# A gMLP that has its gated rows turned by DMA, a third buffer of turned rows, and a filler inside Wo

## The chip, the cores and the metric

One core of one Trainium2 chip. The metric is the device time of one execution in microseconds (us), as a median of runs; all runs here were in the fast state, but for one single run whose state is unknown. A ratio says how one kernel stands to the kernel before, which was run in the same rounds on the same chip: it is the estimate from the runs of both (within 0.0005 of the ratio of their means), so not quite the ratio of the medians quoted beside it. Where I turn a ratio into microseconds, I multiply its distance from 1 by the median of the kernel before in those rounds.

## The reference, cut to what matters

The program applies, twice, a recurrent attention with memory (A) and a gMLP (B), each on layer-normalised rows and each added to its input. To "turn" a tile is to transpose it.

```python
# A: 64 segments of 32 tokens; each sees 8 memory rows which the segment before it wrote
for s in range(n_seg):
    h = jnp.concatenate([mem, xs], axis=1)
    q, k, v = ...                                   # h @ Wq, Wk, Wv
    o = softmax(mask(q k^T * scale)) @ v
    o = jnp.einsum('bhte,hed->btd', o, Wo)
    mem = o[:, :M, :].copy()                        # the recurrence
    ...
# B
z  = _gelu(jnp.einsum('bsd,df->bsf', x, w_in))      # "the projection"
z1 = z[..., :Fh];  z2 = _layernorm(z[..., Fh:])
g  = jnp.einsum('ts,bsf->btf', w_sp, z2) + b_sp     # "the gate", a mix over tokens
return jnp.einsum('bsf,fd->bsd', z1 * g, w_out)     # "w_out"
```

S = 2048 tokens are 16 tiles of 128 rows; Fh = 688.

## The kernel before, the parts that count

In B, the projection takes turned rows from two buffers, a pair of tiles in each; VectorE makes statistics and ScalarE normalises.

```python
def load_rows(self, q):
    lo = KT * FF + 2 * KT * P * (q % 2)             # two buffers
    t = self.take(lo, 2 * KT * P).rearrange(...)
    self.nc.sync.dma_start_transpose(out=t, in_=self.xb_d[2 * P * q:2 * P * (q + 1), :]...)
...
for tt in range(NT):
    project(tt)                                     # 12 matmuls, two gelus on ScalarE, statistics on VectorE
    ...
    if tt % 2 == 1:
        if tt // 2 + 2 < NT // 2:
            front.load_rows(tt // 2 + 2)
        norms(tt // 2, {5: (NT - 4, NT - 3), 9: (NT - 2, NT - 1)}.get(tt, ()))   # late rows of A
        if tt > 1:
            normalise(tt - 3)
            normalise(tt - 2)
```

The gate stage, a tile at a time: 32 gate matmuls into `pg`, a product with z1 on VectorE (`u`), six PE transposes of `u` and two ScalarE copies (`uT`), six matmuls with w_out (`py`).

```python
for t in range(2, NT):
    if t > 2:
        gate(t, range(0, 8))
    turn_u(t - 1)                # six transposes on TensorE
    gate(t, range(8, 13))
    finish(t - 1)                # w_out
    gate(t, range(13, NT))
    product(t)                   # issues the next spatial weight (512 KB, turned by DMA), then u
```

In A, the segments form a chain, and TensorE's waits in it are filled with work that does not belong to it: projections of the next tile's edge rows (`psb`), or Wo of older rows (`pwB`). `fill()` takes the next piece. A segment ends so:

```python
fill()                           # third filler: eight matmuls, two quarters of a psb chunk
... Rm, Rt ...                   # ScalarE: logarithms and exponentials of the sums
for r in range(2):
    nc.vector.tensor_tensor(out=hview(uT_cur[:], r, 0, 8), ...)   # what Wo waits for
    ...
pw = accB.tile([P, 512], F32, name="pw")
wo_pass(pw, uT_cur)              # Wo: 128 small matmuls; writes the memory rows
build_hA(s + 1, pw)
...
fill()                           # fourth filler: sixteen matmuls
```

The softmax here doesn't subtract the row's maximum and nothing guards it: scores larger than these inputs give would overflow.

## Time and profile before

| | before |
|---|---|
| median of 3 runs | 1899.3 us (1897.0 to 1901.9) |
| profiled execution, span | 1886.2 us |
| recurrent block, start to first projection matmul | 800.2 us, then 763.4 us |
| projection, first to first gate matmul | 48.2 us, then 50.4 us |
| gate stage, first gate matmul to start of the last w_out | 110.2 us, then 108.8 us |

Each part of the table is the distance between two starts in TensorE's timeline. TensorE is busy nearly all the time, so these stages simply add up, and a change shows in the stage that it changes. One warning ahead, as it matters later: the profiled execution took 1887.9 us by the clock that times the runs, 9 us less than the fastest of the three.

### The profile page before, as it was taken

Reading aid. Unit: us, or ns where it says so; the run is one execution under the profiler, and the core shown is the slowest. Engines: PE = TensorE matmul, PEld = TensorE weight load, DVE = VectorE, ACT = ScalarE, POOL = GpSimd, SP = SyncE. Lnnn points to the kernel's source line nnn. Section 1 sums busy time; section 2 is a strip of 40 time slices with the busy share of each in tenths; the row PEclk is TensorE's granted clock in tenths of the full one; section 3 lists DMA queues with packets and bytes.
Section 4 is the critical chain, followed back from the end, with each engine's and each line's share of the span. In section 5 each row is a group of like instructions: output and inputs, shape, how many; then the busy total and the mean of one; then the engine's idle time right before and its main releaser. Section 6 shows DMA issues by size and latency. Waiting matters only on the chain.

```text
span 1886.2 us, 94665 instructions
## 1 busy us (share of the span) xinstructions
PE 1761.7 (93%) x43776; PEld 1019.3 (54%) x43776; DVE 1157.8 (61%) x2700; ACT 1139.4 (60%) x2134; POOL 136.8 (7%) x285
## 2 busy tenths in 40 slices
PE   2999999999999999889989999999999999998898
PEld 1555555555555555435545555555555555554455
DVE  2666666676667766584346666666766676666622
ACT  1667766666676666562236776666766676665411
POOL 5000000000000000022010000000000000002000
PEclk9999999999999999999989999999999999999999
DMA  9100000021002101278630000001200120125463
GB/s 349 46 21 19 19 18 18 19 79 30 19 22 76 36 25 32 84 157 161 157 116 21 22 21 21 22 22 46 80 21 21 52 78 25 28 71 148 109 138 95
DMA packets 165269, 119.93 MB, mean 64 GB/s; under 512 B 111896, under 2 KB 140328, under 8 KB 164872
## 3 DMA queue, kind: packets, MB, share of 16 engines
q1 hardware_dynamic: 143016, 65.11, 14.3%
q0 software_dynamic: 10560, 34.07, 5.5%
q10 hardware_dynamic: 11296, 14.70, 2.7%
q8 instruction: 342, 5.60, 1.2%
q14 instruction: 55, 0.45, 0.1%
HBM read 59.29 MB, written 33.56 MB: 49 GB/s over the span
## 4 chain that ended last, share of the span: by engine, by line
PE 85%; DMA 4%; DVE 4%; issue 3%; ACT 2%; POOL 1%; DVEq 0%; SPq 0%; POOLq 0%; ACTq 0%
PE psm L527 23%; PE pw L582 12%; PE psV L527 12%; PE psb L527 10%; PE pg L321 8%; PE psS L684 5%; PE psO L707 4%; PE pwB L594 3%; PE py L347 2%; PE psD L759 2%; PE psM L749 1%; PE pz L261 1%; DMA y_o<-o_d 1%; DMA Wo_sb<-in_A_Wo_dram 1%; PE pT L338 1%
## 5 line engine op out<-in xcount | busy, mean ns | idle before, releaser
L527 PEld LDWEIGHTS <-hA 128*32 128x32 bf16 x12288 | 303.7, 96 | 310.4 <-DVE hA L638 48.4
L663 ACT CAST rows<-psm 128x512 bf16<-128x512 f32 x512 | 300.3, 587 | 192.2 <-PE psm L527 192.2
L582 PE MATMUL pw<-Wo_sb,uT 128*32 128x128 bf16 x16640 | 268.0, 220 | 39.9 <-issue 29.6
L527 PE MATMUL psm<-Wq_sb,hA 128*32 128x512 bf16 x4096 | 274.5, 381 | 12.4 <-DVE hA L638 9.4
L582 PEld LDWEIGHTS <-uT 128*32 128x32 bf16 x16640 | 237.2, 97 | 89.8 <-DVE uT L769 49.8
L527 PE MATMUL psm<-Wk_sb,hA 128*32 128x512 bf16 x4096 | 269.8, 379 | 0.5 <-ACT rowsB L569 0.5
L527 PE MATMUL psV<-Wv_sb,hA 128*32 128x512 bf16 x4096 | 268.0, 382 | 0.0
L667 DVE STREAM_TRANSPOSE QQ<-rows 128x512 bf16<-128x512 bf16 x256 | 182.1, 711 | 78.2 <-ACT rows L663 77.0
L719 DVE TENSOR_TENSOR uT<-psO,Rt 128x384 bf16<-128x384 f32 x256 | 138.6, 541 | 119.0 <-ACT Rt L772 118.7
L688 ACT ACTIVATE E<-psS 128x448 bf16<-128x448 f32 x256 | 140.0, 547 | 117.8 <-PE psS L684 117.8
L667 DVE STREAM_TRANSPOSE KA<-rows 128x512 bf16<-128x512 bf16 x256 | 181.9, 711 | 37.7 <-ACT rows L663 34.3
L769 DVE TENSOR_TENSOR uT<-psO,Rm 128x128 bf16<-128x128 f32 x256 | 62.5, 286 | 163.2 <-PE psD L759 163.2
L321 PE MATMUL pg<-z2n,wspT 128*128 128x344 bf16 x1024 | 160.1, 310 | 0.0
L772 ACT ACTIVATE Rt<-Rt 128x512 f32<-128x512 f32 x256 | 157.6, 630 | 4.1
L684 PEld LDWEIGHTS <-KA 128*64 128x64 bf16 x2048 | 79.7, 113 | 106.1 <-DVE KA L667 106.1
L767 ACT ACTIVATE Rt<-psD 128x1024 f32<-128x1024 f32 x128 | 131.2, 1025 | 5.9
L527 PEld LDWEIGHTS <-hB 128*32 128x32 bf16 x3072 | 79.4, 97 | 96.8 <-issue 27.3
L321 PEld LDWEIGHTS <-wspT 128*128 128x128 bf16 x1024 | 95.3, 98 | 52.2 <-issue 6.8
L691 DVE TENSOR_TENSOR E<-E,maskN 128x448 bf16<-128x448 bf16 x256 | 95.3, 372 | 41.5 <-ACT E L688 41.5
L527 PE MATMUL psb<-Wq_sb,hB 128*32 128x512 bf16 x1024 | 90.5, 394 | 27.0 <-DVE hB L542 27.0
L684 PE MATMUL psS<-QQ,KA 128*64 128x80 bf16 x2048 | 109.9, 208 | 1.1
L744 ACT CAST VA<-psV 128x512 bf16<-128x512 f32 x128 | 75.1, 586 | 56.5 <-PE psV L527 56.5
(136 smaller groups left out, 2283.9 us busy)
## 6 DMA issues: line engine op xcount, KB each, us to landing
Wo_sb<-in_A_Wo_dram POOLq DMA_DIRECT2D x8, 1024.0 KB, 13.1
xs<-xd ACTq DMA_DIRECT2D x32, 256.0 KB
o_d<-o_sb SPq DMA_DIRECT2D x126, 64.0 KB
y_o<-o_d SPq DMA_DIRECT2D x24, 256.0 KB
xd<-y_o SPq DMA_DIRECT2D x22, 256.0 KB
Wq_sb<-in_A_Wq_dram POOLq DMA_DIRECT2D x8, 512.0 KB, 6.9
Wk_sb<-in_A_Wk_dram POOLq DMA_DIRECT2D x8, 512.0 KB, 11.0
Wv_sb<-in_A_Wv_dram POOLq DMA_DIRECT2D x8, 512.0 KB, 11.4
```

Source lines behind the costliest of these rows:

```text
L321: nc.tensor.matmul(pg[t][:, k, 0:344], lhsT=wsp[t][:, st, :], rhs=z2n[:, st, 344 * k:344 * k + 344], start=(st == 0), stop=(st == NT - 1))
L527: nc.tensor.matmul(ps[32 * cg:32 * cg + 32, :], lhsT=lhs(kt, cg), rhs=rhs(kt, cg), start=(kt == 0), stop=(kt == KT - 1), tile_position=(0, ...
L582: nc.tensor.matmul(po[32 * cg:32 * cg + 32, 0:128], lhsT=lhs[:, n, :], rhs=wo_rhs(h, cg), start=(h == 0), stop=(h == H - 1), tile_position ...
L663: nc.scalar.copy(r[:], ps[:])
L667: nc.vector.transpose(out=QQ[:, j % 2, :, 0:32] if j < 2 else KA[:, j % 2], in_=r[:])
L684: nc.tensor.matmul(pS[64 * g:64 * g + 64, i, c0:80 if K is KA else 112], lhsT=K[:, r, n:n + 2, :].rearrange("p h k -> p (h k)"), rhs=q if ...
L688: nc.scalar.activation(out=E[:, r], in_=pS, func=ACT.Exp, scale=scale)
L691: nc.vector.tensor_tensor(out=E[:, r], in0=E[:, r], in1=maskN[:, j4, :].unsqueeze(1).to_broadcast([P, 4, 112]), op=ALU.mult)
L707: nc.tensor.matmul(o if V is VA else ends(o), lhsT=V[64 * g:64 * g + 64, r, i, :], rhs=E[64 * g:64 * g + 64, r, i, c0:c1].rearrange("p (s ...
L719: nc.vector.tensor_tensor(out=hview(uT_nxt[:], r, 8, 32), in0=oview(r, 8, 32), in1=Rr[:, :, :, 0:24], op=ALU.mult)
L767: nc.scalar.activation(out=Rt[:], in_=psD[:], func=ACT.Ln)
L772: nc.scalar.activation(out=rt, in_=rt, func=ACT.Exp, scale=-1.0)
```

## The change

Three changes in one. Six transposes a tile leave TensorE and become one DMA, issued on the queue of the SP engine behind the next spatial weight, and w_out runs a tile later. The turned rows of the projection get a third buffer, and the late rows come earlier. And four of the eight matmuls of the third filler (one of two, where Wo of old rows is the filler) move into the middle of Wo, where I take the aim to be a bridge over Wo's own pauses.

```diff
-        t = self.take(lo, 2 * KT * P).rearrange("p (kt t) -> p kt t", kt=KT)
+        t = self.take(KT * FF + n * (q % 3), n) if q % 3 < 2 else self.rows.tile([P, DM], F32, name="ln_x")[:].bitcast(BF16)
...
-                if tt // 2 + 2 < NT // 2:
-                    front.load_rows(tt // 2 + 2)
-                norms(tt // 2, {5: (NT - 4, NT - 3), 9: (NT - 2, NT - 1)}.get(tt, ()))
+                if tt // 2 + 3 < NT // 2:
+                    front.load_rows(tt // 2 + 3)
+                norms(tt // 2, {5: (NT - 4, NT - 3), 7: (NT - 2, NT - 1)}.get(tt, ()))
...
             if t + 3 < NT:
                 load_wsp(t + 3)
...
+                uT[t] = up.tile([P, 6, P], BF16, name="uT")
+                nc.sync.dma_start_transpose(out=uT[t][:], in_=u[t][:].rearrange("t (fc s) -> t fc s", s=P))
...
-            turn_u(t - 1)
-            gate(t, range(8, 13))
-            finish(t - 1)
-            gate(t, range(13, NT))
+            gate(t, range(0, 10))
+            finish(t - 2)
+            gate(t, range(10, NT))
             product(t)
+        finish(NT - 2)
         turn_u(NT - 1)          # the last tile keeps its PE transposes
...
-                for kts in ((range(0, 1), range(1, 2), range(2, 4)), (range(0, 4),))[k % 2]:
+                for kts in (((0,), (1,), (2,), (3,)), ((0, 1, 2, 3),))[k % 2]:
...
-                if k in (0, 1, 3):
+                if k < 4:
...
+            wo_pass(pw, uT_cur, range(0, H // 2))
+            fill()
+            wo_pass(pw, uT_cur, range(H // 2, H))
...
-            wo_pass(pw, uT_cur)
```

(Cut: pools that make room for the new buffers, the zeroing of the 80 padding columns of `u`, the order of some loads.)

More of the change, by code (lines that the diff above doesn't have):

```diff
@@ L139, with __init__ @@
 class _Front:
-    def __init__(self, nc, pool, xb_d, w_in):
-        self.nc, self.xb_d, self.w_in = nc, xb_d, w_in.rearrange("(kt p) f -> p kt f", p=P)
+    def __init__(self, nc, pool, rows, xb_d, w_in):
+        self.nc, self.rows, self.xb_d, self.w_in = nc, rows, xb_d, w_in.rearrange("(kt p) f -> p kt f", p=P)
         self.space = pool.tile([P, KT * FF + 4 * KT * P], BF16, name="front")
@@ L156, in load_rows @@
     def load_rows(self, q):
-        lo = KT * FF + 2 * KT * P * (q % 2)
-        t = self.take(lo, 2 * KT * P).rearrange("p (kt t) -> p kt t", kt=KT)
+        n = 2 * KT * P
+        t = self.take(KT * FF + n * (q % 3), n) if q % 3 < 2 else self.rows.tile([P, DM], F32, name="ln_x")[:].bitcast(BF16)
+        t = t.rearrange("p (kt t) -> p kt t", kt=KT)
         self.nc.sync.dma_start_transpose(out=t, in_=self.xb_d[2 * P * q:2 * P * (q + 1), :].rearrange("t (kt s) -> t kt s", s=P))
@@ L231, in b_block @@
         wsp_pool = ctx.enter_context(tc.tile_pool(name="b_wsp", bufs=3))
-        zp = ctx.enter_context(tc.tile_pool(name="b_z", bufs=2))
+        zctx = ExitStack()
+        zp = zctx.enter_context(tc.tile_pool(name="b_z", bufs=2))
         ps_pool = ctx.enter_context(tc.tile_pool(name="b_ps", bufs=1, space=PSUM))
@@ L252, in load_wsp @@
         def load_wsp(t):
-            wsp[t] = wsp_pool.tile([P, NT, P], BF16, name="wspT")
+            wsp[t] = wsp_pool.tile([P, NT, P], BF16, name="wspT", tag="wspT")
             nc.sync.dma_start_transpose(out=wsp[t][:], in_=w_sp[t * P:(t + 1) * P, :].rearrange("t (st s) -> t st s", s=P))
@@ L291, in b_block @@
         late_load(NT - 3, gp.tile([P, DM], F32, name="xs", bufs=3)[:], gp.tile([P, DM], F32, name="xo", bufs=1)[:])
-        late_load(NT - 2, gp.tile([P, DM], F32, name="xs", bufs=3)[:], rows.pool.tile([P, DM], F32, name="ln_x")[:])
+        late_load(NT - 2, *(gp.tile([P, DM], F32, name="xs", bufs=3)[:] for _ in range(2)))
+        wl = wsp_pool.tile([P, 2, DM], F32, name="wspL", tag="wspT")
+        late_load(NT - 1, wl[:, 0, :], wl[:, 1, :])
         for tt in range(NT):
@@ L296, in b_block @@
                 load_wsp((tt - 7) // 2)
-            if tt > 13:
-                load_x(tt - 14)
+            if tt == 14:
+                load_x(0)
             if tt % 2 == 1:
-                if tt // 2 + 2 < NT // 2:
-                    front.load_rows(tt // 2 + 2)
-                norms(tt // 2, {5: (NT - 4, NT - 3), 9: (NT - 2, NT - 1)}.get(tt, ()))
+                if tt // 2 + 3 < NT // 2:
+                    front.load_rows(tt // 2 + 3)
+                norms(tt // 2, {5: (NT - 4, NT - 3), 7: (NT - 2, NT - 1)}.get(tt, ()))
                 if tt > 1:
@@ L305, in b_block @@
                     normalise(tt - 2)
-            if tt == 5:
-                late_load(NT - 1)
         normalise(NT - 2)
         normalise(NT - 1)
+        zctx.close()
+        up = ctx.enter_context(tc.tile_pool(name="b_u", bufs=2))
         if out_final is None:
@@ L314, in b_block @@
         pg, u, uT = {}, {}, {}
+        us = [up.tile([P, 6 * P], BF16, name=f"u{i}", bufs=1) for i in range(2)]
+        for i in range(2):
+            nc.gpsimd.memset(us[i][:, FH:6 * P], 0.0)
         def gate(t, sts):
@@ L327, in product @@
                 load_wsp(t + 3)
-            u[t] = gp.tile([P, FH], BF16, name="u", bufs=1)
-            nc.vector.scalar_tensor_tensor(out=u[t][:].rearrange("p (k f) -> p k f", k=2), in0=pg.pop(t)[:, 0:2, 0:344],
+            u[t] = us[t % 2]
+            nc.vector.scalar_tensor_tensor(out=u[t][:, 0:FH].rearrange("p (k f) -> p k f", k=2), in0=pg.pop(t)[:, 0:2, 0:344],
                                            scalar=c["bsp"][:, t:t + 1], in1=z1[:, t, :].rearrange("p (k f) -> p k f", k=2),
                                            op0=ALU.add, op1=ALU.mult)
-            if t + 2 < NT:
-                load_x(t + 2)
+            if t + 1 < NT:
+                load_x(t + 1)
+                uT[t] = up.tile([P, 6, P], BF16, name="uT")
+                nc.sync.dma_start_transpose(out=uT[t][:], in_=u[t][:].rearrange("t (fc s) -> t fc s", s=P))
         def turn_u(t):
@@ L338, in turn_u @@
                 nc.tensor.transpose(pT[0:fsz, fc * P:(fc + 1) * P], u[t][:, f0:f0 + fsz], ident_bf[:])
-            del u[t]
-            uT[t] = gp.tile([P, 6, P], BF16, name="uT", bufs=1)
+            uT[t] = up.tile([P, 6, P], BF16, name="uT")
             nc.scalar.copy(uT[t][:, 0:5, :].rearrange("p fc r -> p (fc r)"), pT[:, 0:640])
@@ L357, in finish @@
             nc.scalar.dma_start(xd[t * P:(t + 1) * P, :], xo[:])
-            _stats(nc, zp, xo[:], MV_out[:, t, :])
+            _stats(nc, up, xo[:], MV_out[:, t, :])
             _rstd_act(nc, RS_out[:, t:t + 1], MV_out[:, t, 1:2], c)
@@ L368, in b_block @@
         gate(1, range(NT - 2, NT))
-        turn_u(0)
         product(1)
-        gate(2, range(0, 6))
-        finish(0)
-        gate(2, range(6, 8))
         for t in range(2, NT):
-            if t > 2:
-                gate(t, range(0, 8))
-            turn_u(t - 1)
-            gate(t, range(8, 13))
-            finish(t - 1)
-            gate(t, range(13, NT))
+            gate(t, range(0, 10))
+            finish(t - 2)
+            gate(t, range(10, NT))
             product(t)
+        finish(NT - 2)
         turn_u(NT - 1)
@@ L441 @@
         rest()
-    front = _Front(nc, ctx.enter_context(tc.tile_pool(name="front", bufs=1)), xb_d, B_w_in)
+    front = _Front(nc, ctx.enter_context(tc.tile_pool(name="front", bufs=1)), rp, xb_d, B_w_in)
     for blk in range(2):
@@ L770, in segment @@
                                         in1=Rm[:, :, r].rearrange("p g (n q) -> p g n q", q=8), op=ALU.mult)
+            pw = accB.tile([P, 512], F32, name="pw")
+            wo_pass(pw, uT_cur, range(0, H // 2))
+            fill()
+            wo_pass(pw, uT_cur, range(H // 2, H))
+            for r in range(2):
                 rt = Rt[:, :, 256 * r:256 * r + 256]
@@ L776, in segment @@
             tok_out(0)
-            pw = accB.tile([P, 512], F32, name="pw")
-            wo_pass(pw, uT_cur)
             if s + 1 < NSEG:
@@ L826, in tail @@
                     front.load_w(j4)
-                    if j4 > 1:
-                        front.load_rows(j4 - 2)
+                    if j4 > 0:
+                        front.load_rows(j4 - 1)
                 if ys:
```

## The prediction

> **What bounds the kernel now.** I read the page's summary first, then the chain of work that ended last, the table of TensorE's waits, and last the timeline in three places: a recurrent segment, the projection of the gMLP, its gate stage.
>
> ```profile
> PE 1761.7 (93%) x43776; PEld 1019.3 (54%) x43776; DVE 1157.8 (61%) x2700; ACT 1139.4 (60%) x2134; POOL 136.8 (7%) x285
> ...
> q8 instruction: 342, 5.60, 1.2%
> ...
> PE 85%; DMA 4%; DVE 4%; issue 3%; ACT 2%; POOL 1%; DVEq 0%; SPq 0%; POOLq 0%; ACTq 0%
> ```
>
> TensorE is busy 93% of the span and holds 85% of the chain, so a change counts only if it takes instructions or waits from TensorE's own stream. Which waits it still has:
>
> ```profile
> PE pw L582 <- issue: 29.6, 46, 1.9
> PE psb L527 <- DVE hB L542: 27.0, 2, 25.9
> PE pz L261 <- DMA front<-xb_d: 16.7, 7, 5.1
> ```
>
> The middle line is the start-up, untouched. The third is the gMLP's projection waiting for turned rows: the change aims at it. The first is Wo waiting for nothing that the profile knows.
>
> One segment, TensorE then VectorE (columns: start us, length us, engine, line, operation):
>
> ```profile
> 408.28 0.62 PE L527 MATMUL psb<-Wv_sb,hB 128*32 128x512 bf16 x8
> 408.73 1.74 PE L582 MATMUL pw<-Wo_sb,uT 128*32 128x128 bf16 x111
> 410.95 0.45 PE L582 MATMUL pw<-Wo_sb,uT 128*32 128x128 bf16 x17 [0.48 <-issue]
> 411.19 1.08 PE L527 MATMUL psb<-Wv_sb,hB 128*32 128x512 bf16 x16
> 412.13 1.05 PE L527 MATMUL psm<-Wq_sb,hA 128*32 128x512 bf16 x16
> ...
> 408.38 0.49 DVE L769 TENSOR_TENSOR uT<-psO,Rm 128x128 bf16<-128x128 f32 x2 [0.81 <-PE psD L759]
> ```
>
> The eight filler matmuls psb start at 408.28 and stream for about 0.43 us; Wo starts at 408.73, when the first of VectorE's two uT products has just ended (0.29 us from 408.38). Wo starts 0.05 us after that product in every filled segment, so the filler is exactly as long as the wait it covers. Wo's gap of 0.48 us has no releaser.
>
> The gate stage, one tile (TensorE has no gap):
>
> ```profile
> 877.07 0.61 PE L338 MATMUL pT<-ident_bf,u 128*128 128x128 bf16 x6
> 877.61 1.63 PE L321 MATMUL pg<-z2n,wspT 128*128 128x344 bf16 x10
> 879.08 1.56 PE L347 MATMUL py<-w_out_sb,uT 128*128 128x512 bf16 x6
> 880.57 3.38 PE L321 MATMUL pg<-z2n,wspT 128*128 128x344 bf16 x22
> 883.79 0.61 PE L338 MATMUL pT<-ident_bf,u 128*128 128x128 bf16 x6
> ```
>
> The period is 883.79 - 877.07 = 6.72 us, of which the six transposes take 877.61 - 877.07 = 0.54.
>
> The projection, and the engines' busy time in it (PE, PEld, DVE, ACT, POOL):
>
> ```profile
> 811.40 9.47 PE L261 MATMUL pz<-front 128*128 128x512 bf16 x48 [1.79 <-DMA front<-xb_d]
> 822.45 9.47 PE L261 MATMUL pz<-front 128*128 128x512 bf16 x48 [1.58 <-DMA front<-xb_d]
> 832.83 4.82 PE L261 MATMUL pz<-front 128*128 128x512 bf16 x24 [0.92 <-DMA front<-xb_d]
> 842.15 6.36 PE L261 MATMUL pz<-front 128*128 128x512 bf16 x24 [4.49 <-DMA front<-xb_d]
> ...
> 806.00:845.00 39.00, 30.23 (x147) 14.20 (x145) 35.40 (x140) 26.88 (x37) 11.36 (x17) 0.96 0.79 170
> ```
>
> Every gap of TensorE ends with turned rows; yet VectorE is busy 35.4 of 39 us. It stands right behind the wait that is removed.
>
> **What the Trainium skill says.** "Runtime: NRT & Kernel Launch", section Instruction fetch mechanics: instructions come in blocks of 16 KiB, 256 at a time, the next being fetched while one runs, and this is said to be mostly hidden. The trace agrees on the blocks (342 fetches, 5.60 MB, 16 KiB each) and not on the hiding: in the first recurrent block Wo's gaps of over 0.25 us nearly all fall on TensorE matmul number 95 modulo 128 (128 matmuls with their weight loads are 256 instructions), and end 1.2 to 1.6 us after such a fetch. Wo runs a whole block in 1.9 us.
>
> "VectorE: DVE Perf Modes", section The three transpose paths, gives a 128x128 bf16 turn as 390 ns on TensorE and 1309 by DMA, and advises TensorE. In the trace the six cost 0.54 us together, pipelined. The longer DMA matters only if it misses its deadline.
>
> "DMA: Bandwidth & Descriptors", section Latency and other measured facts, has 261 GB/s for one transposing kernel. The spatial weight, 512 KB a tile, moves here in about 2.2 us of packets, 240 GB/s: agreed.
>
> "SBUF — State Buffer", section SBUF: two separate sides: VectorE with two SBUF inputs blocks against GpSimd's reads. The trace shows it: a two-column product of VectorE that takes 0.16 us took 2.67 us at 813.04, while GpSimd added late rows.
>
> **The change, part by part.**
>
> *Gate stage.* Fifteen of sixteen tiles lose the six transposes; ScalarE loses two copies a tile, which were off the path. 15 x 0.54 = 8.1 us a block. At the tail, w_out of tile 14 moves out of the last gate into the wait for tile 15's product (TensorE idle 1.57 us there before), which hides about 1.3 us. At the head the first turned tile is late: the SP queue issues the next spatial weight first (about 2.5 us), then the turn (192 KB; 1.23 us is the issue of a 256 KB one, so about 1, an estimate), and it lands some 2 us later, as the row transposes do: about 14.4 us after the stage starts, where w_out asks at 13.0. That loses 1.4 us and replaces about 2 us of start-up waits. Adding up the stage (9.4 us opening, 0.7 wait for the first product, 2.9 + 1.4 + 1.5 + 1.8, then 13 periods of 6.18, then the tail) puts the last w_out at 101.5 us; before it started at 110.2 and 108.8. Sum: -8.7 and -7.3, **-16 us**.
>
> Steady deadline: SP is free about 2.5 us after a gate ends, the turn is issued 1 us later and lands at about 5.5; w_out asks at 6.18 + 2.9 = 9.1. Slack 3.5 us. DMA share goes from 0.76 (mean of the window from 861 to 953 us) to about 0.9 (0.9 us more packets in a period shorter by 0.54).
>
> *Projection.* With three row buffers rows come about one pair of tiles earlier, and the last rows are normalised at tile 7, not 9. TensorE would then need 16 x 2.34 = 37.4 us instead of 48.2 and 50.4. But VectorE needs 4.57 us for a pair (first statistics to next first statistics in the timeline) against TensorE's 4.68, plus about 2.7 for each of two pairs with late rows, plus some 3.5 blocked by GpSimd: about 45.5 us. So only VectorE's idle time at the end goes: 1.54 + 1.14 = 2.7 us in the first block, 2.34 + 1.40 = 3.7 in the second. The gate can start earlier than VectorE ends, since its first eight us do not need the last two tiles: working back through ScalarE's order (normalise pair q before the activations of pair q + 2) I get 844 and 1767 against 848.3 and 1772.3. Less a microsecond of extra blocking, **-9 us** for both.
>
> *Filler quarter in Wo.* Four of the third filler's eight matmuls move into the middle of Wo. The first product of uT, which releases Wo, hangs on ScalarE's and VectorE's chain and comes no earlier; the filler ends 0.21 us sooner, so TensorE idles 0.21 us, then pays the four matmuls inside Wo. Wo ends 0.21 us later. Part returns: after Wo, TensorE now waits about 0.11 us for the copy of the filler's PSUM and for VectorE, so I take 0.17 us. Where Wo or the filler after it stalls on a block fetch anyway (47 of 90 such segments) the fetch's time is absolute and swallows it: 43 x 0.17 = 7.3 us. The 24 segments filled with Wo of old rows lose 0.23 (one more switch between full and tiled array, about 0.1, and 0.13 idle), 16 of them unstalled: 3.7 us. **+11 us.**
>
> Sum: -16 - 9 + 11 = -14. 1899.3 - 14 = **1885 us**.
>
> **The rivals.** (a) The filler breaks up instruction fetch, and the issue waits shrink: then Wo gains up to perhaps 15 us of the 29.6, and the time is 1860 to 1870. Against: the number of instructions is unchanged and four 0.05 us matmuls shift a block by 0.2 us where stalls are 0.4 to 2. (b) The turned u comes late in every tile, because the turn queues behind the 512 KB weight at a DMA share near 0.9: w_out then waits, 1 us a tile would be +30 and the time 1915 to 1925. Against: the slack of 3.5 us. (c) VectorE is not the projection's bound, and all DMA waits go: -22 in place of -9, 1872. Against: its 35.4 busy us of 39. (d) The filler costs nothing, since the wait it covered has slack: 1874. Against: the constant 0.05 us from product to Wo.
>
> **Range and chances.** Gate -10 to -20, projection -3 to -20, filler -5 to +20, and some us either way because the second recurrent block meets the fetch boundaries at another phase (180 instructions fewer before it). Range 1868 to 1900. Over 2% faster needs 1861 or less, the good ends of all three: 0.07. Over 2% slower needs rival (b) at its worst: 0.03.
>
> **What would show it.** Gate period near 6.18 us without transposes and no wait of py on uT beyond the first tile; projection 43 to 46 us long with VectorE's idle gaps gone; Wo with idle time before it, ended by uT, in filled segments, and the unstalled segment 0.17 us longer than the 11.10 us from first psm to first psm that most unstalled ones have now. I am wrong if segments become shorter, if issue waits of Wo halve, if py waits on DMA tile after tile, or if the projection falls under 41 us.

## The result, and the profile after

| | before | after |
|---|---|---|
| median | 1898.2 us (1896.4 to 1901.9, 4 runs) | 1889.0 us (1885.2 to 1891.1, 4 runs) |
| ratio, 95% interval | | 0.9947 (0.9924 to 0.9970) |
| profiled execution, span | 1886.2 us | 1883.4 us |
| recurrent blocks | 800.2, 763.4 us | 807.6, 774.2 us |
| projections | 48.2, 50.4 us | 46.3, 43.4 us |
| gate stages | 110.2, 108.8 us | 105.4, 101.4 us |

A gain of 10 us (6 to 14) where 14 were predicted. The summary page of the changed kernel, its first line of engines and its chain:

```profile
PE 1761.1 (94%) x43572; PEld 1015.0 (54%) x43596; DVE 1162.7 (62%) x2700; ACT 1120.7 (60%) x2074; POOL 136.6 (7%) x289
...
PE 84%; DVE 5%; DMA 4%; issue 3%; ACT 2%; POOL 0%; SPq 0%; ACTq 0%; DVEq 0%; POOLq 0%
```

There are 204 fewer matmul records (180 transposes are gone, as the 180 fewer weight loads say; the other 24 are records missing from the trace) and the chain is still TensorE's. What it waits for (us in total, times, longest):

```profile
PE pw L586 <- issue: 25.9, 41, 1.5
PE pz L263 <- ACT z L266: 10.9, 6, 3.0
...
PE py L357 <- DMA uT<-u: 5.3, 4, 1.5
PE py L357 <- ACT uT L351: 3.7, 2, 2.3
```

The projection's wait for turned rows is gone, and one for ScalarE stands in its place, smaller. w_out waits for its turned rows four times and for the copies of the last tile's transposes twice. In the timeline of the gate stage of block 1 (first line), and of block 2 in a second profile of the same changed kernel (the rest):

```profile
868.35 1.57 PE L357 MATMUL py<-w_out_sb,uT 128*128 128x512 bf16 x5 [1.35 <-DMA uT<-u]
```

```profile
1810.23 1.56 PE L357 MATMUL py<-w_out_sb,uT 128*128 128x512 bf16 x6
1811.72 4.84 PE L329 MATMUL pg<-z2n,wspT 128*128 128x344 bf16 x32
1816.40 1.56 PE L357 MATMUL py<-w_out_sb,uT 128*128 128x512 bf16 x6
```

The period is now 1816.40 - 1810.23 = 6.17 us, without a gap. The first w_out starts 868.35 - 853.92 = 14.4 us after the stage. In the projection (first block, first profile):

```profile
829.33 6.49 PE L263 MATMUL pz<-front 128*128 128x512 bf16 x23 [2.98 <-ACT z L266]
835.68 4.81 PE L263 MATMUL pz<-front,ln_x 128*128 128x512 bf16 x24
842.95 11.14 PE L263 MATMUL pz<-front 128*128 128x512 bf16 x47 [2.46 <-ACT z L266]
```

The rows are there (`ln_x` is the third buffer), but the PSUM that ScalarE has to empty is not. Behind ScalarE stands VectorE: from 813 us to the end of this projection VectorE's timeline has no gap at all.

Last a recurrent segment whose Wo has no pause. The kernel before, which started it at 330.88, then the kernel after, which started its own at 335.08:

```profile
338.80 0.61 PE L527 MATMUL psb<-Wq_sb,hB 128*32 128x512 bf16 x8
339.24 1.97 PE L582 MATMUL pw<-Wo_sb,uT 128*32 128x128 bf16 x128
341.12 1.05 PE L527 MATMUL psb<-Wk_sb,hB 128*32 128x512 bf16 x16
341.98 0.40 PE L527 MATMUL psm<-Wq_sb,hA 128*32 128x512 bf16 x4
```

```profile
342.99 0.40 PE L531 MATMUL psb<-Wq_sb,hB 128*32 128x512 bf16 x4
343.44 1.08 PE L586 MATMUL pw<-Wo_sb,uT 128*32 128x128 bf16 x64
344.34 0.39 PE L531 MATMUL psb<-Wq_sb,hB 128*32 128x512 bf16 x4
344.56 1.07 PE L586 MATMUL pw<-Wo_sb,uT 128*32 128x128 bf16 x64
345.45 1.04 PE L531 MATMUL psb<-Wk_sb,hB 128*32 128x512 bf16 x16
346.37 0.61 PE L531 MATMUL psm<-Wq_sb,hA 128*32 128x512 bf16 x5
```

In both Wo starts 8.36 us into the segment, though the filler ahead of it is half as long now. From Wo's start to the filler behind it the time grew from 1.88 to 2.01 us, from there to the next segment from 0.86 to 0.92. The segment is 346.37 - 335.08 = 11.29 us long in place of 11.10. In each of the 90 `psb` segments of both kernels Wo starts 0.05 to 0.06 us after the end of the first uT product. The idle time ahead of Wo doesn't show as a wait, since the ends of matmuls are modelled (the record has the four end 0.40 us after their start, though the four inside Wo hold it up for 0.22): the waits of `pw` for uT are 8.4 us before and 5.5 after. It is read from the starts.

### The profile page after: what moved, and what is told of

Its sections match the earlier page's. It is cut to its first block, busy times and chain, and to the rows that moved or that the text cites. A ratio compares the mean times of both kernels' runs of the same rounds, so it can differ in the third digit from the quotient of the medians.

```text
span 1883.4 us, 94288 instructions
## 1 busy us (share of the span) xinstructions
PE 1761.1 (94%) x43572; PEld 1015.0 (54%) x43596; DVE 1162.7 (62%) x2700; ACT 1120.7 (60%) x2074; POOL 136.6 (7%) x289
## 4 chain that ended last, share of the span: by engine, by line
PE 84%; DVE 5%; DMA 4%; issue 3%; ACT 2%; POOL 0%; SPq 0%; ACTq 0%; DVEq 0%; POOLq 0%
PE psm L531 24%; PE pw L586 13%; PE psV L531 12%; PE psb L531 8%; PE pg L329 7%; PE psS L688 5%; PE psO L711 4%; PE pwB L598 3%; PE py L357 2%; PE psD L763 2%; PE pz L263 1%; PE psM L753 1%; DMA Wk_sb<-in_A_Wk_dram 1%; DVE uT L773 1%; DMA uT<-u 1%
## 5 line engine op out<-in xcount | busy, mean ns | idle before, releaser
L586 PE MATMUL pw<-Wo_sb,uT 128*32 128x128 bf16 x16640 | 286.1, 219 | 38.2 <-issue 25.9
L586 PEld LDWEIGHTS <-uT 128*32 128x32 bf16 x16640 | 245.2, 97 | 96.3 <-DVE uT L773 46.4
L671 DVE STREAM_TRANSPOSE KA<-rows 128x512 bf16<-128x512 bf16 x256 | 181.9, 710 | 38.3 <-ACT rows L667 35.6
L329 PE MATMUL pg<-z2n,wspT 128*128 128x344 bf16 x1024 | 154.8, 309 | 1.0 <-DVE u L337 1.0
L531 PE MATMUL psb<-Wq_sb,hB 128*32 128x512 bf16 x1024 | 101.3, 396 | 26.9 <-DVE hB L546 26.9
```

The costliest lines, as they stand in the source:

```text
L329: nc.tensor.matmul(pg[t][:, k, 0:344], lhsT=wsp[t][:, st, :], rhs=z2n[:, st, 344 * k:344 * k + 344], start=(st == 0), stop=(st == NT - 1))
L531: nc.tensor.matmul(ps[32 * cg:32 * cg + 32, :], lhsT=lhs(kt, cg), rhs=rhs(kt, cg), start=(kt == 0), stop=(kt == KT - 1), tile_position=(0, ...
L586: nc.tensor.matmul(po[32 * cg:32 * cg + 32, 0:128], lhsT=lhs[:, n, :], rhs=wo_rhs(h, cg), start=(h == 0), stop=(h == H - 1), tile_position ...
L671: nc.vector.transpose(out=QQ[:, j % 2, :, 0:32] if j < 2 else KA[:, j % 2], in_=r[:])
```

## The experiments

Twelve runs, all correct. The first four, on one chip, take the change apart; the next four, on a second chip, test causes; the last four, on a third, settle a disagreement between traces and times.

**1. The filler alone** (the kernel before with this only).

```diff
-                for kts in ((range(0, 1), range(1, 2), range(2, 4)), (range(0, 4),))[k % 2]:
+                for kts in (((0,), (1,), (2,), (3,)), ((0, 1, 2, 3),))[k % 2]:
...
-                if k in (0, 1, 3):
+                if k < 4:
...
-            wo_pass(pw, uT_cur)
+            wo_pass(pw, uT_cur, range(0, H // 2))
+            fill()
+            wo_pass(pw, uT_cur, range(H // 2, H))
```

> The filler quarter alone. Theory: Wo's start hangs on the first uT product, so the quarter taken from ahead of Wo leaves TensorE idle and then delays Wo's end: 11.29 in place of 11.10 us in an unstalled projection-filled segment, 11.77 in place of 11.43 in one filled with Wo of old rows; slower than before by 11 us (the prediction) to 19 us (the trace of the changed kernel), ratio 1.006 to 1.010. Rival: the quarter relieves the instruction fetch; then the issue waits shrink and the ratio is 1 or less.

Measured: 1911.0 us (1907.6 to 1914.9) against 1898.4; ratio 1.0072 (1.0049 to 1.0094), which is 13.7 us slower (9 to 18). The unstalled segment is 11.29 us here too. So this part loses, and the rest of the change wins more than the whole.

**2. The change without the filler** (the changed kernel with the diff of run 1 undone).

> The change without the filler quarter. Theory: both gMLP blocks gain, recurrent blocks as before: 22 to 25 us faster than before, ratio 0.987 to 0.9885, some 1874 us, faster than the changed kernel. Rival (the filler helps or is neutral): no faster than the changed kernel, ratio 0.9947 or more.

Measured: 1873.2 us (1871.3 to 1879.0); ratio 0.9870 (0.9848 to 0.9893): 24.7 us faster, where the prediction's two terms make 25.

**3. The turn by DMA alone** (the kernel before with this, and with the pools and the padded `u` that it needs).

```diff
+                nc.sync.dma_start_transpose(out=uT[t][:], in_=u[t][:].rearrange("t (fc s) -> t fc s", s=P))
...
-            turn_u(t - 1)
-            gate(t, range(8, 13))
-            finish(t - 1)
-            gate(t, range(13, NT))
+            gate(t, range(0, 10))
+            finish(t - 2)
+            gate(t, range(10, NT))
```

> Only the turn of gated rows by DMA. Theory: 15 x 0.54 us of transposes a block and part of the tail go: 12 to 16 us faster, ratio 0.9915 to 0.994; gate period 6.18 us in the second gMLP block. Rival (turned rows come late in every tile): ratio 1 or more.

Measured: 1880.3 us (1875.7 to 1883.7); ratio 0.9907 (0.9884 to 0.9930): 17.7 us faster (13 to 22), more than the 12 to 16 expected. Its two gate stages take 105.5 and 101.1 us, its projections 48.6 and 51.1, as if nothing had been done there.

**4. The third buffer and the earlier late rows alone.**

```diff
+        t = self.take(KT * FF + n * (q % 3), n) if q % 3 < 2 else self.rows.tile([P, DM], F32, name="ln_x")[:].bitcast(BF16)
...
+                if tt // 2 + 3 < NT // 2:
+                    front.load_rows(tt // 2 + 3)
+                norms(tt // 2, {5: (NT - 4, NT - 3), 7: (NT - 2, NT - 1)}.get(tt, ()))
```

> Only the three row buffers and the earlier late rows. Theory: VectorE bounds the projection, so only about 9 us come back, ratio 0.995, and VectorE has no idle gaps in it. Rival (row DMA was the only bound): 22 us, ratio 0.988, projection near 37.4 us in each block.

Measured: 1890.9 us (1886.3 to 1893.5); ratio 0.9961 (0.9939 to 0.9984): 7.4 us faster (3 to 12). Projections 45.4 and 46.0 us. The wait that takes over is again ScalarE's, 15.5 us in eight places. The three parts add up within their noise: 13.7 - 17.7 - 7.4 = -11.4, against -10.1 for the whole.

**5. Without the filler, and the turn issued ahead of the spatial weight.**

```diff
 def product(t):
-    if t + 3 < NT:
-        load_wsp(t + 3)
     ...  # product, then the turn of u
+    if t + 3 < NT:
+        load_wsp(t + 3)
```

> The change without the filler, and the turn of the gated tile issued ahead of the load of the spatial weight on the same queue. Theory: the waits of w_out on turned rows in that kernel (1.77, 1.72, 2.24 us in the first gMLP block, 1.76 in the second) come from the weight's issue standing first (up to 6 us of it in the first block); they nearly vanish, 5 to 7 us faster than the change without the filler, ratio to before about 0.984. Rival: the landing itself is slow; then the waits stay and the ratio is 0.987.

Measured: 1867.9 us (1860.9 to 1871.5) against 1894.9; ratio 0.9852 (0.9825 to 0.9880), 0.0018 or 3.4 us below that of run 2, less than the 5 to 7 expected, and the intervals overlap. The trace is clearer: no w_out waits for its turned rows any longer, and two gate matmuls wait for the weight instead, 2.25 and 1.07 us; the longer:

```profile
875.36 3.09 PE L329 MATMUL pg<-z2n,wspT 128*128 128x344 bf16 x20 [2.25 <-DMA wspT<-in_B_w_sp_dram]
```

The gate stages take 103.3 and 101.2 us, together less than in any of the six profiles with the turn behind the weight (204.5 against 205.7 to 212.0). So the place in the queue decides whether the turn is in time, and the queue has a little room but not much: what comes second can now be late itself. The rival is not refuted, though: by the semaphore events in the packed trace, turns of block 1 still land up to 5.2 us after their issue has ended. An earlier issue leaves time for a slow landing.

**6. Without the filler, and two Newton steps for the reciprocal root in place of three**, which takes three small VectorE instructions from each pair of tiles (0.57 us from the first of a step to the first of the next).

```diff
-    for k in range(3):
+    for k in range(2):
...
-        o = out if k == 2 else pool.tile(...)
+        o = out if k == 1 else pool.tile(...)
```

> The change without the filler, with two Newton steps instead of three in VectorE's reciprocal root: three small VectorE instructions fewer for each pair of tiles, some 4.7 us of VectorE a gMLP block. Theory (VectorE bounds the projection once the rows come early): the projection gets 3 to 4.5 us shorter in each block, 6 to 9 us in all, ratio to before about 0.983, result still correct. Rival (TensorE's activations or the late rows bound it): no change, ratio 0.987.

Measured: 1867.2 us (1863.4 to 1871.1); ratio 0.9851 (0.9823 to 0.9879). Projections 43.0 and 44.0 us where run 2 has 45.3 and 46.1. In run 5, on the same chip, they are 46.2 and 46.1. Nothing but VectorE got less to do, and the projection became shorter by 2.1 to 3.2 us: VectorE is its bound, though TensorE's wait has ScalarE's name. That is less than the 3 to 4.5 us a block that were expected: VectorE's busy time in the projection itself fell only from 37.9 to 35.6 and from 38.1 to 36.1 us (run 2 to run 6). The timed ratio, whose interval holds that of run 2, can't tell.

```profile
PE pz L263 <- ACT z L266: 8.4, 5, 2.7
```

This wait was 12.8 us in run 2.

**7. The filler, and four more matmuls ahead of Wo** (run 1, with a duplicate quarter so that the filler ahead of Wo has eight again; the duplicates overwrite nothing that counts).

```diff
-                for kts in ((range(0, 1), range(1, 2), range(2, 4)), (range(0, 4),))[k % 2]:
+                for n, kts in enumerate((((0,), (0,), (1, 2), (3,)), ((0, 1, 2, 3),))[k % 2]):
```

(Cut: a flag that closes the duplicate's group, and run 1's split of Wo. The lines taken out are those of the kernel before.)

> The filler quarter alone, and four matmuls more in the third filler of each projection-filled segment (a chunk computed twice, result unchanged), so that it is as long as before. Theory (TensorE idles ahead of Wo until the first uT product): the extra matmuls fit into that idle time and cost nothing: 11.29 us for an unstalled segment as with the filler quarter alone, ratio 1.007. Rival (no idle there; the cost is that of breaking Wo up): 0.21 us more in each of 90 segments, ratio 1.015 or more.

Measured: 1913.3 us (1908.5 to 1918.6); ratio 1.0094 (1.0067 to 1.0122), against 1.0072 for run 1, intervals overlapping. An unstalled segment, which started at 383.68:

```profile
391.59 0.62 PE L527 MATMUL psb<-Wq_sb,hB 128*32 128x512 bf16 x8
392.04 1.07 PE L582 MATMUL pw<-Wo_sb,uT 128*32 128x128 bf16 x64
392.94 0.39 PE L527 MATMUL psb<-Wq_sb,hB 128*32 128x512 bf16 x4
393.15 1.07 PE L582 MATMUL pw<-Wo_sb,uT 128*32 128x128 bf16 x64
...
394.96 0.40 PE L527 MATMUL psm<-Wq_sb,hA 128*32 128x512 bf16 x4
```

Wo starts at 8.36 us again and the segment is 394.96 - 383.68 = 11.28 us long, with four matmuls more in it. So in an unstalled segment those four are free: the time ahead of Wo is a wait that has to be filled or lost, and the four moved into Wo left exactly that much idle.

**8. The best of it**: run 2 with the changes of 5 and 6, and at the end of block 1 the two ScalarE operations of tile 14's statistics put behind the last tile's copies.

```diff
-        finish(NT - 2)
+        later = []
+        finish(NT - 2, later)       # its Ln and Exp are put off
         turn_u(NT - 1)
+        for f in later:
+            f()
```

> The change without the filler, with the turn issued first, two Newton steps, and ScalarE's statistics of tile 14 put behind the copies of the last turned tile. Theory: the gains add, with about 1 us from the last: 12 to 17 us faster than the change without the filler, ratio to before 0.979 to 0.981, about 1860 us. Rival: they overlap, 0.984.

Measured: 1860.8 us (1856.4 to 1863.5) against 1894.9; ratio 0.9813 (0.9785 to 0.9841), so unclear at the 2% line but better than both kernels. It is 10.8 us below run 2 by the ratios, short of the 12 to 17 expected, and the rival's 0.984 lies inside the interval. Gate stages 102.6 and 101.1, projections 42.9 and 43.7 us. One wait for turned rows is back in the projection of block 2, 4.0 us.

**9 and 10. The kernel before against itself.** By now traces and times disagreed. From one profile each, the changed kernel's gate stages are 12.2 us shorter, its projections 8.8 shorter, its recurrent blocks 18.2 longer: only 2.8 us gained, as the two spans say, where the times say 10.1.

> The kernel before, unchanged, measured against itself. Open question: in the traces the stages of the changed kernel sum to almost nothing gained (gate stages 11 us shorter, projections 8 shorter, recurrent blocks 19 longer), yet the timed runs gain 10 us. Theory 1: the one profiled execution of the kernel before was a lucky one (1887.9 us where its timed runs have a median of 1898), so its trace understates it; then this copy has a ratio of 1.000 within 0.2%, and its profile shows a span near 1892 to 1900, with the extra time in the recurrent blocks and the projections. Theory 2: the kernel before is handicapped by how it is run beside others; then the copy's ratio is 0.995 or less, its timed runs have a median near 1889, and the gain of the change is really near zero.

> The kernel before once more, for one more profile: by theory 1 a span anywhere between 1887 and 1900; by theory 2 again near 1886.

Measured: 1895.0 us (1889.9 to 1898.5) against 1893.8; ratio 0.9999 (0.9976 to 1.0021). The profiled spans are 1893.0 and 1894.0 us (the second a single run, its state unknown), recurrent blocks 802.4 and 768.5, and 801.1 and 769.1 us. The first theory holds: the comparison is fair, and the first profile of the kernel before was a lucky execution, 5 to 6 us of its luck in the second recurrent block.

**11. The changed kernel again.**

> The changed kernel again, in more rounds. Theory 1: ratio 0.993 to 0.997, as before, and 19 us more in the recurrent blocks than the copies of the kernel before have in theirs only if those are lucky again; against a typical copy some 13 to 15 us. Theory 2: against the copy of the kernel before the ratio is near 0.999.

Measured: 1886.0 us (1884.7 to 1887.9); ratio 0.9957 (0.9936 to 0.9978), 8.1 us faster. Span 1883.9: the changed kernel repeats itself. The recurrent blocks, 806.4 and 775.0 us, are 11 us longer together than those of runs 9 and 10, so short of the expected 13 to 15; against the mean of all ten profiles without the filler they are 14.2 longer.

**12. The turn by DMA alone, again.**

> The turn by DMA alone, again. Its first profile had gate stages of 105.5 and 101.1 us where 110.2 and 108.8 are without it, 12.5 us less, while its timed gain was 17.6 us (interval 13 to 22). If the trace is right and timing noise made the rest, the ratio in these rounds is 0.992 to 0.994; if the timed 17.6 is right, it is 0.990 to 0.991 and something besides the gate stages is shorter by 5 us.

Measured: 1881.0 us (1876.6 to 1886.4); ratio 0.9929 (0.9906 to 0.9952), 13.4 us faster (9 to 18), within the answer set for the case that the trace is right. But its profile shows something that run 3 had only in part: in block 1 the gate stage took 110.7 us, as long as with the transposes; in block 2 it took 101.0. The SP queue of block 1 (issue start, length), and the w_out that needs the turn of its second line:

```profile
888.63 5.06 SPq L255 DMA_TRANSPOSE wspT<-in_B_w_sp_dram  x1
893.79 1.71 SPq L343 DMA_TRANSPOSE uT<-u  x1
895.60 6.39 SPq L255 DMA_TRANSPOSE wspT<-in_B_w_sp_dram  x1
```

```profile
902.45 2.62 PE L356 MATMUL py<-w_out_sb,uT 128*128 128x512 bf16 x6 [4.76 <-DMA uT<-u]
```

VectorE had begun this `u` at 888.64 and ended it within 0.93 us. The turn then stood behind a weight whose issue took 5.06 us, was issued 4.2 us after its data were ready, and landed about 7 us after its own issue ended. By the semaphore events in the packed trace the weight ahead of it landed only at 899.56, 5.9 us after that one's issue had ended, and the turn 2.9 us behind it. In block 2 of the same run no weight's issue took over 2.7 us and w_out waited for a turn only at the start.

## Why the prediction was right, point by point, and where it was off

The measured 1889.0 and 1886.0 us lie inside the range of 1868 to 1900 and within a quarter of a per cent of 1885. That alone says little, as the range takes in the kernel before (1899.3) as well. By the traces all three terms came out less favourable than predicted, so nothing cancelled, and the gain is half of the predicted one; by the times it is 10.1 (6 to 14) and 8.1 (4 to 12) of 14. What was right in the main is the mechanism of each part, and that is shown by the stages. Since one profile can be lucky, I take each stage as the mean over all profiles that share its code (14 in all: ten without the filler and four with it, run 7 with its four extra matmuls among these; seven with two row buffers, five with three and three Newton steps; six with PE transposes, six with the DMA turn behind the weight).

| term | predicted | traces, both blocks | timed |
|---|---|---|---|
| gate stage | -16 | 219.1 to 208.3: -10.8 (the changed kernel's own two: -12.9) | -17.7 and -13.4 (runs 3, 12) |
| projection | -9 | 99.2 to 91.3: -7.9 (own two: -8.5) | -7.4 (run 4) |
| filler | +11 | 1567.2 to 1584.2: +17.1 (own two: +14.4) | +13.7 (run 1; run 7 is +17.8) |
| sum | -14 | own two: -7.0 | -10.1 and -8.1 (result, run 11) |

The traces' own sum of -7.0 agrees with the spans: three profiles of before have a mean of 1891.1, two of after 1883.7, so -7.4.

**Gate stage: the mechanism right, block 2 right in size, block 1 not.** The period of 6.18 us and the late first turn at 14.4 us came as predicted, and block 2's 101.4 us as well (101.5 predicted). Block 1 took 105.4 and 104.5 us. The step that failed is the steady deadline, in both its terms: "SP is free about 2.5 us after a gate ends", and "lands at about 5.5", some 2 us after the issue, which made "Slack 3.5 us". In block 1 of the changed kernel the weights' issues took 1.9 to 6.1 us, in block 2 2.0 to 2.9; the long ones eat the slack, two w_outs waited (1.21 and 1.49 us), and in run 12 one waited 4.76. The second of the two in the changed kernel, with the turn that it needs:

```profile
896.37 1.24 SPq L344 DMA_TRANSPOSE uT<-u  x1
902.25 1.57 PE L357 MATMUL py<-w_out_sb,uT 128*128 128x512 bf16 x6 [1.49 <-DMA uT<-u]
```

The gate had ended and the product begun at 891.71. The turn was issued 4.7 us later in place of 2.5, and landed at 10.5 in place of 5.5, 4.6 us after its issue had ended; w_out asked at 9.05, as predicted (9.1). For the other wait the turn was issued at 3.4 and landed at 9.4, in run 12 at 5.2 and 13.8. So the slow landing took more of the slack than the late issue. That is rival (b), in one or two tiles of block 1 and not in every one. Run 5 confirms that an earlier place in the queue removes the waits; in run 8, with the same order, one w_out still waited 0.85 us. Why the issues and landings are longer in block 1 no run isolates; the weights' issues reach 4.1 us there in the kernel before already, against 2.6 in block 2. Block 1's gate stage also loads the next block's rows, and its DMA engines were busy for 0.90 of the window from 868 to 955 us against 0.82 in block 2 (1791 to 1876), which fits, but that is argued and not shown. Block 1's tail is longer as well: its last w_out waits 2.32 us for ScalarE's copies, block 2's 1.42, as ScalarE has tile 14's statistics to do first in block 1 alone. Run 8 puts these off, and the two waits fall from 3.7 us together to 2.8.

**Projection: right.** 46.3 and 43.4 us, in the second profile 45.9 and 45.7, where 43 to 46 was predicted (the 43.4 is the lowest of five profiles of this code in block 2, the others being 45.7 to 46.1); VectorE's idle gaps are gone; run 6 shows VectorE to be the bound. Rival (c), that all waits go, falls: they changed their name from a DMA to ScalarE and kept two thirds of their size (16.7 to 10.9 us). The reader of a profile would take ScalarE for the bound here; it only stands between.

**Filler: the sign and the mechanism right, the size short.** The prediction's unstalled segment was 0.17 us longer; it is 0.19. For the segments filled with Wo of old rows it had 0.23; they went from 11.43 to 11.77 us, so 0.34. It had counted "one more switch between full and tiled array, about 0.1, and 0.13 idle". In the trace the piece inside Wo takes 0.32 us from its start to Wo's second half, the stretch ahead of Wo falls only from 0.54 to 0.44, and Wo's two halves take 1.01 us each where the whole took 1.90: these last 0.12 us are what it left out. With no absorption that makes 90 x 0.19 + 24 x 0.34 = 25.3 us, where the prediction's sizes make 20.8. The second half is the absorption by stalls: the prediction let 47 of 90 and 8 of 24 segments swallow the cost, 9.8 us of it; over all profiles the `psb` segments grew by 12.7 us and the `pwB` segments by 4.9 (17.6 together, where the whole blocks give 17.1), so 7.7 of the 25.3 were swallowed. The mis-sized term is thus mainly the cost of a segment, above all of the second kind, by 4.5 us, and for the rest the absorption, by 2. The timed runs, +13.7 with an interval of 9 to 18, cannot tell 17 from 11; the traces can.

**Rival (a)**, that the filler relieves Wo's pauses, falls, though with a grain of truth. Wo's waits of the kind "issue" are 31.3 us as a mean of the ten profiles without the filler (29.3 to 34.8) and 24.2 with it (21.7 to 26.1): 7.1 less. But the same kind of wait at the psb matmuls rises from 7.3 to 10.8, presumably as the block boundaries that fell into Wo fall into the filler now. What goes in truth is 3.6 us, and the recurrent blocks are 17.1 us longer all the same. **Rival (d)**, that the filler is free, falls by runs 1 and 7.

**What the prediction did not see** is the noise of a single profile. It took all its numbers from an execution whose second recurrent block was 5 to 6 us shorter than two further ones had it. None of its steps rests on that length, so it did no harm to the sum; it did harm to my first comparison of the traces. What stays open is a difference of some 5 us between the timed gain of the turn (-15.5 as a mean of its two measurements) and its traces (-10.8). The intervals of the two reach down to 13 and 9, and block 1's gate stage alone varies from 104.5 to 110.7 us between profiles of the turn, so it may be nothing more than that; I have not shown it.

## What to carry to other kernels

A piece of filler belongs into a wait that really exists: moved from in front of a dependency to the middle of a stream that runs, it cost nearly its whole length here (0.19 of 0.21 us in an unstalled segment), and what it left behind was idle. When work is moved from the bounding engine to a DMA, look at what is issued ahead of it on the same queue, and put the transfer with the nearest deadline first; and reckon the landing, not only the issue, as it is under load. And before stages of two single profiles are subtracted, profile the kernel before once more: here two executions of one program differed by 7 us, nearly as much as the change gained.

## What the Trainium skill lacked or had wrong

- "VectorE: DVE Perf Modes", section Rules for kernel authors, recommends TensorE for a 128x128 turn when PSUM is fine as its target. Here TensorE is the bound and the DMA has a tile's time to spare: moving 15 of 16 tiles to the DMA was 13.4 to 17.7 us faster (ratios 0.9929 and 0.9907). The advice lacks the question which engine is free.
- "Runtime: NRT & Kernel Launch", section Instruction fetch mechanics, calls the cost of a block boundary mostly hidden. In Wo, whose matmuls start some 15 ns apart, the waits without a releaser, which in the first block lie nearly all at one place of the 256-instruction grid, are 29.3 to 34.8 us of an execution in ten profiles; and splitting Wo moved 3.5 of the 7.1 us that it lost into the neighbouring matmuls.
- No page that I read tells how long transposing DMAs of these sizes hold the queue that issues them, or how that grows under load; cycle counts for "previous generations" stand in "DMA: Bandwidth & Descriptors", beside those of a later chip. In the gate stages of all runs here the issue of a 192 KB one took 1.2 to 2.4 us, of a 512 KB one 1.6 to 6.4 us, and all those over 3.2 us lie in block 1, which loads the next block's rows meanwhile.
